# A spectral mixing layer times a gated GLU on one core: the first pair of GLU blocks by seven products, five pairs' first two products moved ahead, tokens 512-1023 by features, and one order table

## The chip, the core and the metric

The kernel runs on one core of one Trainium2 chip. The core has five engines with a queue each: TensorE (PE, matmuls, with its weight loads shown as PEld), VectorE (DVE), ScalarE (ACT), GpSimd (POOL) and SyncE (SP). SP and POOL issue nearly all DMA transfers. The metric is device time of one execution in microseconds (us); lower is better.

## What is computed

```
def _A_ref(x, ...):                       # x: 1 x 2048 x 512
    a = einsum("bsd,ed->bse", x, dft_hid_re)
    b = einsum("bsd,ed->bse", x, dft_hid_im)
    return einsum("ts,bse->bte", dft_seq_re, a) - einsum("ts,bse->bte", dft_seq_im, b)

def _B_ref(x, w_gate, w_up, w_down):      # F = 1792
    g = einsum("bsd,df->bsf", x, w_gate)
    u = einsum("bsd,df->bsf", x, w_up)
    return einsum("bsf,fd->bsd", sigmoid(g) * u, w_down)

xn = layernorm(x)
out = x + _A_ref(xn, ...) * silu(_B_ref(xn, w_gate, w_up, w_down))
```

All values are float32. The numbers S = 2048 tokens, D = 512 features, F = 1792 hidden columns.

## The kernel before, in words

**Precision.** Each matmul operand is split into a high part (ACT copies it to the matmul's reduced type, `split`, line 86) and a low part (DVE subtracts, line 87). A product is then three matmuls, high x high, high x low, low x high (`mm3`, lines 90 to 92), each 128 x 128 weights by up to 512 columns.

**Seven for eight.** A 2 x 2 block product is made of seven products of sums of blocks instead of eight of the blocks. The sums (lines 142 and 270) and the additions of results (`snap`, `plus`, `seed` in `block`) are work for DVE and ACT. A product number 1 to 7 names one of the seven, in the usual scheme: 1 and 2 use blocks as they are, 5, 6, 7, 3 and 4 use sums.

**The GLU.** F is cut into seven groups of 256 columns, g = 0 to 6, and the tokens into two halves, h = 0 and 1. A pair of a half and a group is a block of `BLOCKS`, fourteen with (0, 0). In `block` one product (`unit`) is 12 matmuls of 512 columns: two matrices (gate and up), two pieces of the contraction, three matmuls each. Banks of PSUM are named by matrix and chain: ga, ua, gb, ub, gc, uc, and two named pd. Behind a product stands one product of the earlier pair with w_down (`Seven.run`, six matmuls into pd); its result is copied by ACT and added in DRAM by a POOL transfer with accumulation (`gather`, lines 327 to 332, into g_part).

**The start.** The first pair, (0, 0), is not made by `block` but by `start` (line 520): eight products of the blocks themselves (`chunk`, line 541), with no sums of weights or x. Those on tokens 0-511 run in two halves of 256 columns. The tokens of the first half, 0-1023, are loaded in eight tiles of 128 (`fetch`), normalised (`norm_a` statistics, `norm_b`), transposed on PE (`turn`, line 231) and read out of PSUM three times (`keep_hi`, `keep_lo`, `keep_raw`). Filler matmuls on ones (`busy`) stand ahead of it. A string, `HEAD`, writes out the order of this part.

**The other tokens.** For tokens 1024-2047 x is not transposed. The host also passes x by features (x_t); the moments of the tokens go to DRAM (m_part), come back spread over all partitions, and DVE applies them (`turned_half`, line 217).

**Later stages.** After the fourteen pairs come the sequence DFT (`seq_units`), by seven products on two levels, and the hidden DFT with the gate (`hidden_units`).

**What sets the order.** Each queue runs in the order in which the program issues. Products are `units`; operands are loaded `LOAD_AHEAD` units ahead and split `SPLIT_AHEAD` ahead, or at places given by tables of offsets (S0, H0, S4, H4, LATE). Each page of SBUF has a home from a string, `HOMES`.

Of the kernel before, what the change touches and what calls it, by code (L numbers as in the profile page):

```python
# [15 lines left out]
P = 128  # L16
S, D, F = 2048, 512, 1792
NS = S // P
ND = D // P
# [7 lines left out]
BLOCKS = (*((0, g) for g in range(1, 7)), (1, 6), *((1, g) for g in range(6)))  # L27
# [3 lines left out]

HOMES = (
    "ab10cdiejfghZYXklmnoptqursvwxyzABCDEFGHIJKLMNOPQR1ST0XUVWoxmcftDwkplArsBnJzZISETYWHtRfmDylNAkvMQnBZE"
    "IzKLS0wWRCf1mXDyvckTnpZzESlRCJHtKm1MDQXNLcnBpYEZAzIKCyJ01QMLSpfXTBkzAEHtIlNJmMQvLpSRBDEkKIctNMfYLp0R"
    "BJ1DzAEXmcHMfCyYpLTlJ1AkQmXHC0SidTtMNAGFJDkzRfje0ESKTPOIdBcFVUQNyRxopknuqtlLIHfCB1AcFGvZQXjyRJnimkxz"
    "ICMYGD0ceuydJRviqZxmNCMBYt0GDRFdzJxcijqYMe0ntVURNdFDHfzuCcYqvI0MeyZDRfNJzBuCYIteGMiqjRDZdfFVvzYCHxIU"
    "etGnjRcdNz0FVYxMUyeBuCtncDNZdiHkFMfxJyqeBuvczDdHIMkJCeGqVYufvcNzZtxHiJk0enGqFfzDvtHmyiknqVfBOFPI0MtS"
    "DvEcHNYeTyKnagVZpfodOBuLlMqtmvJGAH10NxeXFnQZVzprwuBiKkGLJmvHjS0A1lDVZpxzwUkiGmJHvLAl1pxGiYzvHLUlGxSA"
    "YiHKvzlULRjxGtiYzvwbhASRNFLYisWwCbhAzYSDLscilFgbCOzAsLicFlfCgbodsiLwlFEobfiswFlAEowsfaFlTyAswaflLAyw"
    "slfSyAzsWwflyESYoszCwLWgflbEyiUdYFSTo0swzLvhgalfbWkUiEAyOSYDdCTcs0LzrhgkWiUDbYECdscL0kWUiEYrdfLCa0UW"  # L40
    "EDilrYAgyCa0EWkFliUAYDoygwE0sCkFfvilODYSyohwgs0ETfFiWvDOySkhwA0sCfTadiFYDvLUIPSyAbgwsCTfiMdqYFrnULQo"
    "cSPbOAewXgTCBfiuzvqdFZkVYInr0UJamLDoPOQybHKSslweCGTtXuiBEvq1pMAFdWjYgxVchLmyRNQHbs0rkKwlXCeEBvq1ZFAU"
    "SdMpPTmJLVgxaKkGf0QNszeCWtZ1dSOcIpnMPL"
)


@with_exitstack
def fnet_glu_kernel(ctx: ExitStack, tc: tile.TileContext, x, x_t, c_re, c_im, w_h, w_gu, w_down, out):
    nc = tc.nc
# [9 lines left out]
    def page(shape, dtype=F32R):  # L59
        return pages.tile([P, *shape], dtype, name="page", tag=next(homes))  # L60

    def bank(tag):
        return banks.tile([P, 512], F32, name=tag, bufs=2 if tag == "pd" else 1)

    ident = const.tile([P, P], F32, name="ident")
    make_identity(nc, ident)
# [6 lines left out]
    moments = const.tile([P, 2, 2, KH // 2], F32, name="moments")  # L73
# [4 lines left out]
    m_part = dram.tile([2, 2, P, KH // 2], F32, name="m_part")  # L78
# [103 lines left out]
    def norm_a(i):  # L182
        st = stats[:, i % 4, :]
        rs = stat.tile([P, 1], F32, name="rs")
        mv = moments[:, i % KH // 4, :, i % 4] if i >= KH else stat.tile([P, 2], F32, name="mv")
        nc.vector.bn_stats(st[:, :6], xs[i])
        nc.vector.bn_aggr(mv, st)
        mean, scale = mv[:, 0:1], mv[:, 1:2] if i >= KH else rs
        nc.gpsimd.tensor_tensor(scale, mv[:, 1:2], mhalf, op=ALU.pow)
        if i >= 4:  # L190
            nc.gpsimd.tensor_scalar(shifts[:, i - 4 : i - 3], mean, scale, -1.0, op0=ALU.mult, op1=ALU.mult)
        st_of[i] = mean, scale

    def second_norm(i):
        i_ = i - KH
        scale, bias = moments[:, i_ // 4, 1, i_ % 4 : i_ % 4 + 1], shifts[:, i - 4 : i - 3]
        nc.scalar.activation(xs[i], xs[i], AF.Identity, scale=scale, bias=bias)

    def norm_b(i):
        mean, scale = st_of.pop(i)  # L200
        if i >= 4:
            nc.scalar.activation(xs[i], xs[i], AF.Identity, scale=scale, bias=shifts[:, i - 4 : i - 3])
            return
        nc.vector.tensor_scalar(xs[i], xs[i], mean, scale, op0=ALU.subtract, op1=ALU.mult)

    def turned_half(n, b, at):

        both = Load(m_part[b].rearrange("m q o -> (m q o)").partition_broadcast(P).rearrange("p (m t) -> p m t", m=2), [2, SB])
        raw = [Load(x_t[(2 + b) * 2 + j], [2, SB]) for j in range(2)]

        def store():
            nc.gpsimd.dma_start(m_part[b].rearrange("m q o -> q m o"), moments[:, b])

        def step(j, m):
            v = xraw[1, j, b] = raw[j].load()
            by = both.load()[:, m, :].unsqueeze(1).to_broadcast([P, 2, SB])
            nc.vector.tensor_tensor(v, v, by, op=(SUB, ALU.mult)[m])

        after(n, store)
        sooner(at[0] - 2, both.load)  # L220
        for i in range(4):
            if i % 2 == 0:
                sooner(at[i] - 4, raw[i // 2].load)
            after(at[i], lambda i=i: step(*divmod(i, 2)))
# [3 lines left out]
    def turn(i):  # L228
        turned[i] = bank({2: "ga", 3: "ua"}.get(i, "pd")).rearrange("p (d s) -> p d s", d=ND)
# [62 lines left out]
    def w_operands(g):  # L292
# [19 lines left out]
        w["s"] = s1, s2, s3, s4  # L312
        return w
# [25 lines left out]
    HEAD = "C000 C001 C002 T2 S4 C010 H2 C011 T3 S5 H3 C012 R2 C100 C101 R3 N4 L2 L3 T4 u0 N5 H4 S6 R4 L4 C102 T5 S7 g00 R5 H5 C110 U0 N6 V0 L5 N7 T6 C111 d0 u1 C112 T7 H6 g01 p2 H7 L6 u2 L7 U1 h1 V1 m R7 R6 C200 x1 C201 C202 p3 C210 h2 X5 d1 g10 C211 u3 x2 d2 C212 d3 X6 g11"  # L339
    S0 = 8, 10, 8, 14  # L340
    H0 = 13, 11, 11, 12
    L4 = 9, 13, 15, 20
    S4 = 9, 7, 8, 12
    H4 = 8, 9, 11, 14
    X34 = 0, 0
    SEVEN_LAST = (1, 2, 6, 7, 4, 5, 3)
    waiting = []

    class Down:
# [22 lines left out]
        def spread(self, n, late):  # L372
            sooner(n + 4 * late - 4, self.wdl.load)
            for i, f in zip(LATE if late else (0, 2, 3, 5), (lambda: self.diffs(0), lambda: self.diffs(1), self.dif.get, self.raw.get)):
                after(n + i, f)

    class Seven:


        items, at = SEVEN, range(7)  # L380
# [18 lines left out]
        def spread(self, n, late):  # L399
# [3 lines left out]
            self.last = n == 7 * (len(BLOCKS) - 1)  # L403
            for i, v in zip(L4 if self.last else S0 if n < 0 else S4, self.sums):
                sooner(n + i, v.get)
            if not self.last:
                for i, v in zip(H0 if n < 0 else H4, (self.h[5], self.h[6], self.h[7], self.h[4])):
# [42 lines left out]
    def block(h, w, made, before, job, late, order=(1, 5, 2, 6, 7, 4, 3)):  # L450
# [3 lines left out]
        if not made:  # L454
            for i, v in zip((-2, -3, 0, 1), w["s"]):
# [25 lines left out]
        tail = {1: seed, 6: lambda: snap(2), 7: lambda: (snap(3), plus(3)), 3: lambda: plus(2)}  # L481
        CH = {1: "a", 5: "c", 2: "b", 6: "a", 7: "a", 4: "a", 3: "c"}

        def unit(k, d, parts=(0, 1)):
            first = k in (1, 5)
            for m in parts:
# [4 lines left out]
            if 1 not in parts:  # L491
                return
            if k in tail:
                tail[k]()
            if d:
                d[0].run(d[1])
# [7 lines left out]
        for i, k in enumerate(order):  # L504
            if i == 2:
                waiting.extend((before, d) for d in before.items)
            d = waiting.pop(0) if waiting and i in waiting[0][0].at else None
            add([xop[h, k], w[k]] + (d[0].needs(d[1]) if d else []), lambda *m, k=k, d=d: unit(k, d, m or (0, 1)))
        if order[1] == 2:
            job.product_two = lambda: times(1, "b")  # L510
        else:
            sooner(n + 3, lambda: times(1, "b"))
        sooner(n + 5, lambda: times(3))
        sooner(n + 7, lambda: times(2))
# [3 lines left out]
    following = []  # L518

    def start(h, g):  # L520

        loads = [Load(w_gu[g, k], [2, 4 * P]) for k in range(2)]
        down = Down(g)
        w, ps = {}, {}
        job = Seven(h, down, True)
        job.items = SEVEN_LAST
        job.spread(-7, False)

        def w_hi(f, j):
            k, o = QUAD[f, j]  # L530
            both = page([2, 4 * P])
            w[f, j] = both[:, 0], both[:, 1]
            nc.scalar.activation(both[:, 0], loads[k].load()[:, o, :], AF.Copy)

        def w_lo(f, j):
            k, o = QUAD[f, j]
# [698 lines left out]
```

## Time and profile before

| | |
|---|---|
| time, three runs (us) | 798.49, 799.17, 796.92; median 798.49 |
| span of the profiled execution (us) | 795.6 |
| PE clock granted | 1.00 throughout |
| HBM read, written (MB) | 104.86, 70.26 |
| POOL busy (us) | 121.9 (15%) |

The profile is of one execution. Its own whole time is not given beside it; the span runs from the first to the last instruction and is 2.9 us under the median. A busy share says how long an engine had work, not that the work was needed at once. Since PE stands at 99%, the rows to look at are PE's own pitch and, for the other engines, idle time in a stretch.

### The profile page before, as it was taken

How to read it: one execution, taken by the hardware profiler on the slowest of the kernel's cores; microseconds unless marked ns; L12 is line 12 of the kernel's file. 1: busy time of each engine (PE TensorE's matmuls, PEld its weight loads, DVE VectorE, ACT ScalarE, POOL GpSimd, SP SyncE). 2: the span in 40 equal slices, each digit the busy share in tenths (PEclk: the TensorE clock that was granted, in tenths of full speed). 3: DMA queues.
4: the chain of work that ended last, by engine and by line, in shares of the span. 5: the costliest groups of instructions: out<-in, count | busy, mean ns of one | idle time of the engine just before them, and what ended most of it. 6: DMA issues, size and time to landing. Idle time of an engine off the chain costs nothing.

```text
span 795.6 us, 10166 instructions
## 1 busy us (share of the span) xinstructions
PE 789.4 (99%) x3540; PEld 655.2 (82%) x3540; DVE 710.0 (89%) x925; ACT 543.6 (68%) x844; POOL 121.9 (15%) x173
## 2 busy tenths in 40 slices
PE   9999999999999999999999999999999999999997
PEld 8888888888888888888888888888888888888886
DVE  7899889899988988988988898899889899889987
ACT  5778888888877877978987747554544455449461
POOL 2003341111221312212110000101100000000102
PEclk9999999999999999999999999999999999999999
DMA  7058899887887899988998788829968684876836
GB/s 285 7 183 213 182 215 209 183 183 114 190 200 202 218 229 263 247 197 192 228 297 277 171 279 263 251 68 329 393 252 312 207 295 167 296 274 232 185 59 106
DMA packets 49571, 172.11 MB, mean 216 GB/s; under 512 B 5488, under 2 KB 5744, under 8 KB 49520
## 3 DMA queue, kind: packets, MB, share of 16 engines
q0 software_dynamic: 20128, 69.75, 41.7%
q1 hardware_dynamic: 29312, 101.66, 36.1%
q8 instruction: 27, 0.44, 0.2%
q14 instruction: 24, 0.20, 0.1%
q10 hardware_dynamic: 80, 0.07, 0.0%
HBM read 104.86 MB, written 70.26 MB: 220 GB/s over the span
## 4 chain that ended last, share of the span: by engine, by line
PE 99%; DVE 0%; ACT 0%; issue 0%
PE ga L91 6%; PE pd L91 6%; PE pd L92 6%; PE ga L92 6%; PE ga L90 6%; PE pd L90 6%; PE ua L92 6%; PE ua L91 6%; PE ua L90 6%; PE gb L92 4%; PE gb L91 4%; PE gb L90 4%; PE ub L92 4%; PE ub L91 4%; PE ub L90 4%; PE uc L92 4%
## 5 line engine op out<-in xcount | busy, mean ns | idle before, releaser
L87 DVE TENSOR_TENSOR page<-page 128x1024 fp32r<-128x1024 f32 (+2 forms) x408 | 370.8, 944 | 46.3 <-ACT page L86 44.9
L86 ACT ACTIVATE page<-page 128x1024 fp32r<-128x1024 f32 (+2 forms) x408 | 319.0, 834 | 130.4 <-DVE page L142 116.0
L142 DVE TENSOR_TENSOR page<-page 128x512 f32<-128x512 f32 (+2 forms) x280 | 223.9, 820 | 1.7
L327 ACT ACTIVATE page<-pd 128x512 f32<-128x512 f32 x140 | 81.9, 599 | 37.4 <-PE pd L92 31.8
L329 POOL DMA_DIRECT2D g_part<-page x76 | 65.7, 865 | 271.9 <-ACT page L327 244.7
L91 PE MATMUL ga<-page 128*128 128x512 f32 x200 | 77.9, 390 | 0.0
L91 PE MATMUL pd<-page 128*128 128x512 f32 x200 | 77.9, 390 | 0.0
L90 PE MATMUL ga<-page 128*128 128x512 f32 x200 | 77.9, 389 | 0.0
L92 PE MATMUL pd<-page 128*128 128x512 f32 x200 | 77.8, 389 | 0.0
L92 PE MATMUL ga<-page 128*128 128x512 f32 x200 | 77.8, 389 | 0.0
L90 PE MATMUL pd<-page 128*128 128x512 f32 x200 | 77.8, 389 | 0.0
L90 PE MATMUL ua<-page 128*128 128x512 f32 x196 | 76.3, 389 | 0.0
L91 PE MATMUL ua<-page 128*128 128x512 f32 x196 | 76.3, 389 | 0.0
L92 PE MATMUL ua<-page 128*128 128x512 f32 x196 | 76.2, 389 | 0.0
L90 PE MATMUL gb<-page 128*128 128x512 f32 (+1 forms) x140 | 53.7, 384 | 0.0
L92 PE MATMUL gb<-page 128*128 128x512 f32 (+1 forms) x140 | 53.6, 383 | 0.0
L91 PE MATMUL gb<-page 128*128 128x512 f32 (+1 forms) x140 | 53.6, 383 | 0.0
L91 PE MATMUL ub<-page 128*128 128x512 f32 x132 | 51.4, 389 | 0.0
L90 PE MATMUL ub<-page 128*128 128x512 f32 x132 | 51.4, 389 | 0.0
L92 PE MATMUL ub<-page 128*128 128x512 f32 x132 | 51.4, 389 | 0.0
L90 PE MATMUL gc<-page 128*128 128x512 f32 x124 | 48.2, 389 | 0.0
L91 PE MATMUL gc<-page 128*128 128x512 f32 x124 | 48.2, 389 | 0.0
(152 smaller groups left out, 1288.0 us busy)
## 6 DMA issues: line engine op xcount, KB each, us to landing
g_part<-page POOLq DMA_DIRECT2D x84, 512.0 KB, 6.3
page<-in_c_re_dram SPq DMA_DIRECT2D x49, 512.0 KB, 5.0
page<-in_c_im_dram SPq DMA_DIRECT2D x33, 512.0 KB, 5.6
page<-in_w_gu_dram SPq DMA_DIRECT2D x26, 512.0 KB, 5.5
f_part<-page POOLq DMA_DIRECT2D x16, 512.0 KB, 6.6
page<-f_part SPq DMA_DIRECT2D x16, 512.0 KB, 4.7
page<-i_part SPq DMA_DIRECT2D x14, 512.0 KB, 4.5
page<-in_w_down_dram SPq DMA_DIRECT2D x13, 512.0 KB, 4.9
```

The costliest lines, as they stand in the source:

```text
L86: nc.scalar.activation(hi, src, AF.Copy)
L87: nc.vector.tensor_tensor(lo, src, hi.bitcast(F32), op=SUB)
L90: nc.tensor.matmul(ps, ws[0], ms[0], start=first, stop=False, skip_group_check=go_on)
L91: nc.tensor.matmul(ps, ws[0], ms[1], start=False, stop=False, skip_group_check=go_on)
L92: nc.tensor.matmul(ps, ws[1], ms[0], start=False, stop=last, skip_group_check=go_on)
L142: (engine or nc.vector).tensor_tensor(dst, a, b, op=op)
L327: nc.scalar.activation(pg[:, o, :], po, AF.Copy, scale=float(sign))
L329: nc.gpsimd.dma_start(g_part[i], pg, accum_op=ADD)
```

## The change

It has five parts.

1. The pair (0, 0) becomes an ordinary block of `BLOCKS`, made by seven products. `start` and its `chunk` over eight products go.
2. For the first `AHEAD` = 5 pairs, products 1 and 2 are made ahead of all others, by a new class `Ahead`. They need only tokens 0-511. For pairs 0 and 1 they run in halves of 256 columns, as the tiles arrive. The result of product 1 is kept in SBUF (`keep`; for pair 0 in its bank) and put back into bank ga and ua by ACT after product 5 (`again`). These five pairs then have five units each (`SHORT`).
3. The products with w_down of the first pairs are put off: `COUNTS` says how many follow each unit, none at first, then one and two in turn.
4. Tokens 512-1023 are taken from x by features, as those of the second half were (`Turned`). Their moments go through m_part too; their token order within the block changes as in the other blocks, on the host (`columns`).
5. The kernel records every instruction (`Recorder`, `Ref`) and issues them in the order of one table of numbers (`ORDER`, `emit`). `HOMES` is new as well. All instructions of the changed kernel therefore have one line, that of `emit` (L326).

```diff
-BLOCKS = (*((0, g) for g in range(1, 7)), (1, 6), *((1, g) for g in range(6)))
+BLOCKS = (*((0, g) for g in range(7)), (1, 6), *((1, g) for g in range(6)))
+AHEAD = 5
...
+0 15-16 72 5 20 3 31 1 6 4 19 7 9 21 8 11 29 13 10 22 12 14 74 23 32 73 24 26 33 25 36 27 30 108 28 35 176
...
+def emit(program, order):
...
+    for part in order.split():
+        first, _, last = part.partition("-")
+        for f, a, k in program[int(first) : int(last or first) + 1]:
+            f(*map(found, a), **{n: found(v) for n, v in k.items()})
...
+        def step(self, j, m):
+            h, b = divmod(self.q, 2)
+            v = xraw[h, j, b] = self.raw[j].load()
+            by = self.both.at[:, m, :].unsqueeze(1).to_broadcast([P, 2, SB])
+            nc.vector.tensor_tensor(v, v, by, op=(SUB, ALU.mult)[m])
...
+    SHORT = 5, 6, 7, 3, 4
+    COUNTS = "00000 00012 12121 21212 21212 1111111 1111111"
...
+        def again():
+            for m, c in enumerate("gu"):
+                if kept.g == 0:
+                    ps[c + "a"] = kept.ps[1][m]
+                else:
+                    ps[c + "a"] = bank(c + "a")
+                    nc.scalar.activation(ps[c + "a"], kept.first[:, m, :], AF.Copy)
...
+    class Ahead:
...
+        BANK = "a", "c", "b", "c", "pd"
...
+        def chunk(self, k, n, q):
+            at = (slice(0, 2 * P), slice(2 * P, SB), slice(0, SB))[q]
...
+            for m in range(2):
+                for kt in range(2):
+                    o = (2 * m + kt) * P
+                    nc.tensor.matmul(
+                        self.ps[k][m][:, at],
+                        self.w[k].at[u][:, o : o + P],
+                        xop[0, k].at[v][:, kt, at],
...
+        def keep(self, q):
...
+            for m in range(2):
+                to = self.first[:, m, at] if self.g else self.ps[2][m][:, at]
+                nc.scalar.activation(to, self.ps[1][m][:, at], AF.Copy)
...
-            d = waiting.pop(0) if waiting and i in waiting[0][0].at else None
+            d = [waiting.pop(0) for _ in range(min(len(waiting), counts[n + i] if n + i < len(counts) else 1))]
...
-    def start(h, g):
...
+        emit(program, ORDER)
```

Where it moves instructions, three places. PE first, from the filler matmuls on (ones) over the transposes of the first two token tiles (ident) to the first useful products. Before:

```order
L569 MATMUL gc<-ones 128x512 x10
L231 MATMUL pd<-ident,page 128x128 x4
L569 MATMUL gc<-ones 128x256 x2
L231 MATMUL pd<-ident,page 128x128 x4
L569 MATMUL gc<-ones 128x256 x4
L550 MATMUL gb<-page 128x256 x2
L550 MATMUL ub<-page 128x256 x2
```

The same place after the change, from the last of the ten wide fillers on:

```order
L326 MATMUL ub<-ones 128x512 x3
L326 MATMUL pd<-ident,page 128x128 x4
L326 MATMUL gb<-ones 128x256
L326 MATMUL pd<-ident,page 128x128 x4
L326 MATMUL ua<-page 128x256 x2
L326 MATMUL ub<-ones 128x256
L326 MATMUL gb<-ones 128x256 x2
L326 MATMUL ub<-ones 128x256
L326 MATMUL ua<-page 128x256 x2
L326 MATMUL ga<-page 128x256 x6
L326 MATMUL ub<-ones 128x256
L326 MATMUL gc<-page 128x256 x2
```

One narrow filler now stands ahead of the first useful product instead of six; the others stand between useful ones.

ACT, from the start of the program to the reads of the third and fourth token tile (pd to page are reads of a transposed tile, page to page splits of weights). Before:

```order
L72 ACT_TABLE_LOAD
L72 ACTIVATE warm<-mhalf 128x1
L533 ACTIVATE page<-page 128x512
L250 ACTIVATE page<-pd 128x2x128 x4
L533 ACTIVATE page<-page 128x512 x3
L242 ACTIVATE page<-pd 128x2x128 x4
L250 ACTIVATE page<-ga 128x2x128 x2
L250 ACTIVATE page<-ua 128x2x128 x2
```

After:

```order
L326 ACT_TABLE_LOAD
L326 ACTIVATE page<-page 128x512 x2
L326 ACTIVATE page<-pd 128x2x128 x5
L326 ACTIVATE page<-page 128x512
L326 ACTIVATE page<-pd 128x2x128
L326 ACTIVATE page<-page 128x512
L326 ACTIVATE gb<-ga 128x256
L326 ACTIVATE ub<-ua 128x256
L326 ACTIVATE page<-pd 128x2x128 x2
L326 ACT_TABLE_LOAD
L326 ACTIVATE warm<-mhalf 128x1
L326 ACTIVATE page<-pd 128x2x128 x6
```

The load for the sigmoid, which stood first, is now a second load behind the reads of the first two tiles; copies that seed bank gb and ub stand ahead of it.

DVE, at the place where tokens 512-1023 become operands. Before, it takes their low parts out of PSUM, tile by tile (pd):

```order
L256 TENSOR_TENSOR page<-pd,page 128x2x128 x2
L87 TENSOR_TENSOR page<-page 128x512
L256 TENSOR_TENSOR page<-pd,page 128x2x128 x2
L87 TENSOR_TENSOR page<-page 128x512
L479 TENSOR_TENSOR page<-page,ub 128x512
L270 TENSOR_TENSOR page<-page 128x1024
```

After, it applies the moments to the pages loaded by features (here with the tiles' numbers: 392 holds the moments, 295 and 312 the two halves of x) and goes on to sums of x:

```order
L326 TENSOR_TENSOR page_312<-page_312,page_392 128x1024
L326 TENSOR_TENSOR page_295<-page_295,page_392 128x1024
L326 TENSOR_TENSOR page_312<-page_312,page_392 128x1024
L326 TENSOR_TENSOR page_295<-page_295,page_392 128x1024
L326 TENSOR_TENSOR page_483<-page_312,page_181 128x1024
```

Eight reads in pieces of 2 x 128 columns became four operations of 1024, behind a wait for m_part's way through DRAM; over the whole program DVE has 5 operations of 1024 columns and 11 of 512 more, and 8 of 2 x 128 fewer.

More of the change, by code (lines that the diff above doesn't have):

```diff
@@ L312, in w_operands @@
         w["s"] = s1, s2, s3, s4
+        w["loads"] = loads
         return w
@@ new lines, in fnet_glu_kernel @@
+    job = last = None
+    ahead = []
+    for h, g in BLOCKS:
+        made = g == last
+        if not made:
+            w, wd, last = w_operands(g), Down(g), g
+        new = Seven(h, wd, made)
+        kept = None
+        if len(ahead) < AHEAD:
+            kept = Ahead(g, w, new.s)
+            ahead.append(kept)
+        order = STEADY if not kept else SHORT if g < AHEAD - 1 else (5, 6, 7, 4, 3)
+        job = block(h, w, made, job, new, (h, g) != BLOCKS[-1], order, kept)
+    for i, f in zip(X0, (lambda: x_sum(0, 3), lambda: x_sum(0, 4), xop[0, 7].get, xop[0, 3].get, xop[0, 4].get)):
+        sooner(i, f)
```

651 lines of the change are left out of this document (434 added, 217 removed).

## Prediction

> **What bounds the kernel now.** I read the page's busy shares and chain first, then the PE waits, then the PE timeline of the opening and of the end, and last the windows, for the engine that stands second.
>
> ```profile
> span 795.6 us, 10166 instructions
> PE 789.4 (99%) x3540; PEld 655.2 (82%) x3540; DVE 710.0 (89%) x925; ACT 543.6 (68%) x844; POOL 121.9 (15%) x173
> PE 99%; DVE 0%; ACT 0%; issue 0%
> PE gc L569 <- DVE ones L68: 1.4, 1, 1.4
> ```
>
> PE is busy for 99% of the span, the chain of work is PE alone, and its only named wait is the first 1.4 us. So time goes where matmuls go, as long as nothing new makes PE wait. The rows of the PE timeline (start, length, instruction) give the pitches and the few waits that are there.
>
> ```profile
> 6.58 0.78 PE L569 MATMUL gc<-ones 128*128 128x256 f32 x2
> 7.16 0.69 PE L231 MATMUL pd<-ident,page 128*128 128x128 f32 x4
> 7.60 0.72 PE L569 MATMUL gc<-ones 128*128 128x256 f32 x4
> 8.32 0.50 PE L550 MATMUL gb<-page 128*128 128x256 f32 x2
> 8.66 0.39 PE L550 MATMUL ub<-page 128*128 128x256 f32 x2
> 9.11 0.50 PE L550 MATMUL gb<-page 128*128 128x256 f32 x2
> ...
> 17.57 0.60 PE L231 MATMUL pd<-ident,page 128*128 128x128 f32 x4
> 17.92 0.48 PE L550 MATMUL gb<-page 128*128 128x256 f32 x2
> 18.24 0.40 PE L550 MATMUL ub<-page 128*128 128x256 f32 x2
> 18.48 0.40 PE L550 MATMUL gb<-page 128*128 128x256 f32 x2
> ...
> 20.35 0.40 PE L90 MATMUL ga<-page 128*128 128x512 f32 x1
> ...
> 50.66 0.49 PE L91 MATMUL pd<-page 128*128 128x512 f32 x1
> 50.98 0.40 PE L92 MATMUL pd<-page 128*128 128x512 f32 x1
> ```
>
> ```profile
> 778.85 0.39 PE L92 MATMUL ub<-page 128*128 128x512 f32 x1
> ...
> 785.20 0.28 PE L90 MATMUL gb<-page 128*128 128x256 f32 x1
> ...
> 790.69 0.28 PE L92 MATMUL gb<-page 128*128 128x256 f32 x1
> ```
>
> - A 512-wide matmul: 28 begin between 778.85 and 785.20, so 0.2268 us each. A 256-wide pair takes 0.24 (18.24 to 18.48), so 0.12 each.
> - Four transposes: from 17.57 the second pair behind them begins at 18.24; less one pair that is 0.43.
> - Waits of PE now: from 8.32 to 20.35 are 40 pairs (9.6) and four groups of transposes (1.72), together 11.3 of 12.0 us: 0.7 of waits, two of them visible (9.11 instead of 8.90) and one more of 0.1 at 50.66. Over everything from 8.32 to the last matmul at 790.69, 3372 x 0.2268 + 120 x 0.12 + 6 x 0.43 leaves the same 0.8.
>
> The windows show who stands second (columns: window, its length, busy time of PE, PEld, DVE, ACT, POOL with counts, clock, DMA share, GB/s).
>
> ```profile
> 0.00:20.00 20.00, 18.47 (x118) 16.71 (x119) 14.44 (x36) 11.86 (x31) 5.68 (x18) 1.00 0.79 284
> 20.00:40.00 20.00, 20.00 (x104) 16.99 (x103) 17.72 (x31) 15.16 (x30) 1.14 (x4) 1.00 0.02 7
> 40.00:60.00 20.00, 20.00 (x89) 16.32 (x88) 19.15 (x29) 14.83 (x27) 1.84 (x3) 1.00 0.54 184
> 60.00:80.00 20.00, 20.00 (x90) 16.55 (x89) 19.42 (x34) 17.37 (x31) 7.71 (x11) 1.00 0.88 213
> 80.00:100.00 20.00, 20.00 (x90) 16.55 (x89) 17.36 (x31) 16.74 (x29) 5.86 (x8) 1.00 0.88 184
> ```
>
> DVE is idle for 5.6, 2.3, 0.9, 0.6 and 2.6 us: 11.9 us in the first 100, of which 3.0 lie before its first data.
>
> ```profile
> 3.45 0.69 DVE L186 BATCH_NORM_STATS2 stats<-page 128x6 f32<-128x512 f32 x1 [2.06 <-DMA page<-in_x_dram]
> 110.03 0.69 DVE L142 TENSOR_TENSOR page<-page 128x512 f32<-128x512 f32 x1
> 110.64 0.69 DVE L479 TENSOR_TENSOR page<-page 128x512 f32<-128x512 f32 x1
> 782.41 2.35 DVE L87 TENSOR_TENSOR page<-page 128x1024 fp32r<-128x1024 f32 x2
> ```
>
> DVE operations follow each other at 0.60 us (512 wide) and 1.13 (1024 wide, 2.35 less 1.22 of the last).
>
> **What goes from PE.** Seven products of 12 matmuls stand where eight stood: 12 x 0.2268 = 2.7 us. Tokens 512-1023 are no longer transposed: four groups at 0.43 = 1.7 us. Counted in the two orders that is 3540 matmuls to 3512, and the 120 of 256 columns stay 120. Together **4.4 us**. The end of the program, from the last pieces of the output on, stands in PE's queue as before: nothing there.
>
> **What comes back, the fillers.** Before, all six 256-wide filler matmuls ran ahead of the first useful one (6.58, 7.60), where PE waited anyway. Now five of the six stand behind it: 5 x 0.12 = **0.6 us**, if PE has work there; nothing, if they fill waits of the next paragraph, so I count them once. The start itself I leave at 8.3: it hangs on the second transpose and one read by ACT, as before. ACT now splits a second weight block ahead of them, inside the time in which it would wait for that transpose.
>
> **What comes back, the opening.** Here ACT is the short engine.
>
> ```profile
> 6.25 0.63 ACT L533 ACTIVATE page<-page 128x512 fp32r<-128x512 f32 x1 [4.03 <-DMA page<-in_w_gu_dram]
> 7.88 0.66 ACT L250 ACTIVATE page<-pd 128x256 fp32r<-128x256 f32 x2 [0.26 <-PE pd L231]
> 9.70 1.41 DVE L256 TENSOR_TENSOR page<-pd,page 128x256 fp32r<-128x256 f32 x4
> 10.40 1.15 ACT L533 ACTIVATE page<-page 128x512 fp32r<-128x512 f32 x2 [1.35 <-DMA page<-in_w_gu_dram]
> 493.64 1.28 ACT L947 ACT_TABLE_LOAD   x1
> 495.05 2.22 ACT L86 ACTIVATE page<-page 128x1024 fp32r<-128x1024 f32 x2
> ```
>
> A read of a transposed tile takes 0.33, a weight split 0.63, and where ACT and DVE read one bank they take turns (0.35 each). I lay ACT's queue end to end from 7.9. The copy that seeds product 2 of the first pair follows six reads and two splits and ends at 11.0; PE, with 16 useful matmuls and five fillers since 8.3 (21 x 0.12), is there at 10.8: a wait of 0.3 with the signal. Then ACT loads a table in mid-stream; the second load of before shows its price, 493.64 to 495.05 = 1.4 us with the small activation behind it. The tiles of tokens 256-511 are read behind it at 14.7, PE wants them at 14.2: 0.5. The copy of pair 1's first product ends at 15.9, PE is there at 15.4: 0.5. With a few restarts of 0.1 that is 1.5 us of waits against 0.7 now: **0.8 us** back.
>
> On that table load the Trainium skill ("ScalarE: Activation LUTs", What ACT_TABLE_LOAD costs) says about 1.28 us and then a drain of about 1.38, so 2.66 for a switch of sets. The trace agrees with the 1.28 and shows no drain: the next wide activation begins 1.41 after the load. By the page the third wait would be 1.4 us longer, and the sum the same amount less good; I go by the row.
>
> **What must be covered: DVE.** By the order, DVE gets 5 more operations of 1024 columns (x by features: subtract and multiply), 11 more of 512 (weight sums and splits of the first pair) and 8 fewer of 256: 5 x 1.13 + 11 x 0.60 - 8 x 0.34 = 9.5 us, nearly all in the first 100 us, where 11.9 - 3.0 = 8.9 were idle after the first data. So the cover is the whole idle time of DVE. I added DVE's queue up to each operand that PE waits for. After 98.7 us of products PE needs an operand that stands 103.9 us deep in DVE's queue, 103.3 of it behind 3.45. PE is there at 8.3 + 98.7 + 1.5 = 108.5, so DVE has 105.05 us: 1.75 to spare, and the turns with ACT in the opening take 1.6 of it. The same margin, 0.1 to 0.5 us, stands at some twenty places between 24 and 108 us. For before the same sum has 42.7 us of queue for the matmul at 50.66, plus 7.9 idle by the windows (none between 40 and 50): 50.6, and that row shows PE waiting 0.1. The sum can be trusted to some tenths.
>
> So each further wait of DVE there is a wait of PE, though not added up: the longest lateness counts. Who can be late are transfers.
>
> ```profile
> g_part<-page POOLq DMA_DIRECT2D x3, 512.0 KB, 6.0
> DMA to landing us min/median/max: 2.0/3.7/7.2
> ```
>
> The first row is the issues from 60 to 70 us, median to landing; the second is all four transfers of m_part. Between the first gather and the ACT instruction that waits for its page stand 22 matmuls, 5.0 us: about 1 us late by the 6.0. The moments of tokens 512-1023 leave POOL at about 20.7 by the same laying out; store and load at the median end at 20.7 + 3.7 + 3.7 = 28, wanted by DVE at 29.3; a load of 7.2 would be 2.3 late. Of all this I take **0.4 us**, between nothing and 3: most landings are covered by ACT's lead. The three added loads (two of x_t, one of m_part) and POOL's store stand in the DMA's empty time (0.02 from 20 to 40).
>
> **Sum.** -4.4 + 0.6 + 0.8 + 0.4 = -2.6 on a span of 795.6. The median of the runs is 2.9 above the span, which stays. 798.5 - 2.6 = **795.9 us**, 0.33% less.
>
> **Rivals.**
> - *Little is given back.* The fillers lie in the waits, the loads that are no longer held back land sooner, DVE is never late: -4.4 + 0.3 = 794.4. For it: x and weights are issued in one row from 0.7 on. Against it: ACT's queue is long whatever the loads do. Chance 0.20.
> - *DVE's cover breaks.* A moments transfer 2.3 late, or gathers 1.5 to 3 late, stop DVE inside its full stretch: -3.0 + 2.5 = 798.0. For it: margins of tenths over 80 us. Against it: with 0.88 of the DMA taken from 60 to 100, nearly all the idle time ahead of DVE's largest group is put down to ACT (row below), none to a transfer. Chance 0.19.
> - *The table load holds ACT longer* where it stands in the opening, by as much again as the load itself (1.28): 795.9 + 1.3 = 797.2. Against it the row at 495.05. Chance 0.04. The Trainium skill's drain is this case.
> - *The gathers choke: slower.* The deferred last products run 23 in 15 units of the third to fifth pair (15 x 2.72 + 23 x 1.36 = 72 us), 3.1 us apart, where before had one per 4.1. The last but one gather of a pair and the first of the next write the same part of g_part, and POOL, in order, waits for the earlier to land: two gathers on, 6.2 us. With a landing over 6.2 it waits; at the 8.2 of the row below it is 2 us at each of four joints. If pages and pd banks are held that long, PE stops 8 us less the cover of 1: 795.9 + 7 = 803. It decides from a landing of some 7 us on. For it: 8.2 has been seen. Against it: with 8.2 PE did not wait. Chance 0.09.
>
> ```profile
> L87 DVE TENSOR_TENSOR page<-page 128x1024 fp32r<-128x1024 f32 (+2 forms) x408 | 370.8, 944 | 46.3 <-ACT page L86 44.9
> ...
> g_part<-page POOLq DMA_DIRECT2D x2, 512.0 KB, 8.2
> ```
>
> (The second row is the issues from 100 to 110 us.)
>
> That the change does not do what it says I exclude: the matmuls are counted in the order.
>
> **How the numbers follow.** Forecast 0.48, 795.0 to 796.8. With 0.20 at 794.4, 0.23 at 797 to 798.6 and 0.09 at 803, a range from 793.8 to 798.6 leaves out the last and little more. Faster by over 0.3% (about what a measurement of this kernel can tell from none) means under 796.1: all of 794.4 and two thirds of the forecast, 0.52. Slower by over 0.3% is 0.09; the rest, 0.39, is within.
>
> **What would show it.** PE has 3512 matmuls and, behind 8.3, under 2 us of idle, all before 25 us; DVE is 97% busy from 20 to 108 and the PE waits name DVE there with tenths. The first useful matmul stands at 8.3. If PE's waits name DVE with more than 2 us in all, the cover was the error; if idle POOL time shows g_part in long pieces and PE waits for pd, the gathers; if the opening's waits on ACT are over 2, the table load or the loads' crowding. If the last matmul begins before 787 I gave back too much.

## The result and the profile after: 2.7% slower

| | before | changed |
|---|---|---|
| median (us) | 797.88, 4 runs | 818.22, 4 runs (817.83 to 821.73) |
| ratio to before | | 1.0267, interval 1.0245 to 1.029 |
| span of the profiled execution (us) | 795.6 | 816.3 |
| first useful matmul, begin of the last (us) | 8.32, 790.69 | 8.28, 788.91 |

The forecast was 795.9 us, and the range ended at 798.6. The page of the changed kernel answers to the rows of before (span, share of the engines, chain of work):

```profile
span 816.3 us, 10116 instructions
PE 786.3 (96%) x3512; PEld 650.7 (80%) x3512; DVE 716.3 (88%) x933; ACT 543.0 (67%) x851; POOL 126.4 (15%) x174
PE 90%; DVE 3%; DMA 2%; ACT 1%; POOL 1%; issue 1%; POOLq 0%; SPq 0%; DVEq 0%; ACTq 0%
```

PE has 3.1 us less busy time and ends earlier, as forecast, yet its share of the span falls from 99% to 96%. So PE's queue did not get longer: the span did, behind it. The windows of the end (window, length, busy time of PE, PEld, DVE, ACT, POOL with counts, clock, DMA share, GB/s) show the changed kernel's last 76 us:

```profile
740.00:760.00 20.00, 20.00 (x90) 16.58 (x89) 19.19 (x19) 9.47 (x11) 0.00 (x0) 1.00 0.07 27
760.00:780.00 20.00, 20.00 (x89) 16.55 (x89) 15.99 (x17) 11.55 (x14) 0.00 (x0) 1.00 0.00 1
780.00:800.00 20.00, 9.18 (x52) 7.89 (x50) 8.52 (x14) 0.00 (x0) 7.92 (x8) 0.78 0.36 67
800.00:816.00 16.00, 0.00 (x0) 0.00 (x0) 0.00 (x0) 0.00 (x0) 1.26 (x2) 0.50 0.99 179
```

For 40 us the DMA engines stand nearly still, and POOL does nothing. Then the DMA is 0.99 busy for 16 us in which no engine computes. The granted clock of 0.78 and 0.50 stands only where PE has nothing left to do; up to 789 us, where PE starts its last matmul, it is 1.00. What moves so late, POOL's timeline says (start, length, instruction, idle time ahead and what ended it). The kernel before:

```profile
737.61 1.24 POOL L1056 DMA_DIRECT2D out_dram<-page  x1 [19.19 <-DVE page L1047]
744.13 1.21 POOL L1056 DMA_DIRECT2D out_dram<-page  x1 [5.28 <-DVE page L1055]
...
782.79 1.20 POOL L1056 DMA_DIRECT2D out_dram<-page  x1 [3.38 <-DVE page L1055]
786.39 0.90 POOL L1050 DMA_DIRECT2D out_dram<-page  x1 [2.40 <-DVE page L1049]
787.80 0.87 POOL L1050 DMA_DIRECT2D out_dram<-page  x1 [0.51 <-DVE page L1096]
```

The changed kernel:

```profile
715.48 0.56 POOL L326 DMA_DIRECT2D f_part<-page  x1 [11.22 <-ACT page L326]
792.08 9.18 POOL L326 DMA_DIRECT2D out_dram<-page  x8 [76.04 <-DVE page L326]
```

Before, the eight stores that add a block to `out` left one by one from 737.6 on. Now all eight stand in one row from 792.1 on: POOL waited 76 us for the first. Its queue in the changed kernel, with the pages' numbers, shows why:

```
168 DMA f_part<-page_6430 128x1024
169 DMA out<-page_6851 128x512      (second half of the last but one block)
170 DMA out<-page_6629 128x2x512    (before: the first store of all)
171 DMA out<-page_6572 128x2x512
172 DMA out<-page_6823 128x2x512
173 DMA out<-page_6544 128x2x512
174 DMA out<-page_6745 128x2x512
175 DMA out<-page_6917 128x2x512
176 DMA out<-page_6851 128x512      (first half of the last but one block)
```

Row 169 waits for page 6851. Of the six whole blocks behind it the first is done at about 737 us, and five are done 8 us or more before 6851; they wait. The input of row 169 is itself late, as DVE's timeline of the changed kernel shows:

```profile
789.22 0.42 DVE L326 TENSOR_TENSOR page<-page,gb 128x256 f32<-128x256 f32 x1 [3.75 <-PE gb L326]
789.55 1.02 DVE L326 TENSOR_TENSOR page<-page 128x256 f32<-128x256 f32 x2
790.49 0.68 DVE L326 TENSOR_TENSOR page<-page,ub 128x512 f32<-128x512 f32 x1
791.09 1.62 DVE L326 TENSOR_TENSOR page<-page 128x512 f32<-128x512 f32 x3
792.63 0.68 DVE L326 TENSOR_TENSOR page<-page,pd 128x512 f32<-128x512 f32 x1
```

Before, the multiplications of this block stood at 785.39 and 786.72. Now the one that row 169 needs is the first of the three at 791.09, behind a row that waits 3.75 us for PE's very last bank; and a multiplication out of a pd bank, whose last matmuls start at 750.77 by PE's timeline, comes last of all. In the order table these entries (nine of them: 5315, 5349, 5388, 5424, 5557, 5588, 5619 and 5622 for POOL, 5423 for DVE) stand at its end. None is waited for by anything but a store or the end of the program.

### The profile page after: what moved, and what is told of

The parts are those of the page before. It is cut to its first block, busy times and chain, and to the rows that moved or that the text cites. A ratio compares the mean times of both kernels' runs of the same rounds, so it can differ in the third digit from the quotient of the medians.

```text
span 816.3 us, 10116 instructions
## 1 busy us (share of the span) xinstructions
PE 786.3 (96%) x3512; PEld 650.7 (80%) x3512; DVE 716.3 (88%) x933; ACT 543.0 (67%) x851; POOL 126.4 (15%) x174
## 4 chain that ended last, share of the span: by engine, by line
PE 90%; DVE 3%; DMA 2%; ACT 1%; POOL 1%; issue 1%; POOLq 0%; SPq 0%; DVEq 0%; ACTq 0%
PE ga L326 16%; PE pd L326 16%; PE ua L326 16%; PE gb L326 11%; PE gc L326 11%; PE ub L326 11%; PE uc L326 11%; DVE page L326 3%; DMA g_part<-page 1%; POOL out_dram L326 1%; ACT page L326 1%; DMA page<-in_w_gu_dram 1%; DVE stats L326 0%; POOL moments L326 0%; ACT L326 0%
## 5 line engine op out<-in xcount | busy, mean ns | idle before, releaser
L326 DVE TENSOR_TENSOR page<-page 128x512 fp32r<-128x512 f32 (+5 forms) x756 | 628.0, 889 | 56.0 <-ACT page L326 47.5
L326 ACT ACTIVATE page<-page 128x512 fp32r<-128x512 f32 (+3 forms) x452 | 350.3, 823 | 130.5 <-DVE page L326 109.2
L326 PE MATMUL pd<-page 128*128 128x512 f32 x624 | 158.9, 390 | 0.1
L326 PE MATMUL ga<-page 128*128 128x512 f32 (+1 forms) x606 | 156.7, 387 | 0.2 <-ACT page L326 0.2
L326 PE MATMUL ua<-page 128*128 128x512 f32 (+1 forms) x594 | 154.0, 387 | 0.9 <-ACT page L326 0.9
L326 PEld LDWEIGHTS pd<-page 128*128 128x128 f32 x624 | 116.9, 188 | 25.5 <-ACT page L326 1.3
L326 PEld LDWEIGHTS ga<-page 128*128 128x128 f32 x606 | 113.2, 188 | 23.6 <-ACT page L326 0.4
L326 PEld LDWEIGHTS ua<-page 128*128 128x128 f32 x594 | 110.9, 188 | 24.1 <-ACT page L326 1.2
L326 POOL DMA_DIRECT2D g_part<-page x84 | 70.5, 862 | 317.1 <-ACT page L326 293.8
L326 ACT ACTIVATE page<-pd 128x512 f32<-128x512 f32 (+2 forms) x161 | 89.6, 577 | 36.0 <-PE pd L326 30.9
L326 PE MATMUL gc<-page 128*128 128x512 f32 (+1 forms) x420 | 110.8, 384 | 0.1
L326 PE MATMUL uc<-page 128*128 128x512 f32 (+1 forms) x420 | 110.4, 383 | 0.0
L326 PE MATMUL gb<-page 128*128 128x512 f32 (+1 forms) x420 | 109.6, 381 | 0.2 <-ACT gb L326 0.2
L326 PE MATMUL ub<-page 128*128 128x512 f32 (+1 forms) x396 | 105.9, 386 | 0.0
L326 PEld LDWEIGHTS gc<-page 128*128 128x128 f32 x420 | 78.0, 188 | 16.1 <-ACT page L326 0.6
L326 PEld LDWEIGHTS uc<-page 128*128 128x128 f32 x420 | 77.9, 188 | 15.6 <-DVE page L326 0.2
L326 PEld LDWEIGHTS gb<-page 128*128 128x128 f32 x420 | 76.9, 188 | 15.8 <-ACT gb L326 0.8
L326 PEld LDWEIGHTS ub<-page 128*128 128x128 f32 x396 | 73.8, 188 | 15.0
L326 ACT ACTIVATE page<-ga 128x512 f32<-128x512 f32 x51 | 30.5, 597 | 12.2 <-PE ga L326 11.5
L326 POOL DMA_DIRECT2D f_part<-page x16 | 8.9, 558 | 176.8 <-DVE page L326 152.1
L326 ACT ACTIVATE page<-gb 128x512 f32<-128x512 f32 x32 | 19.1, 596 | 24.1 <-PE gb L326 23.2
L326 ACT ACTIVATE page<-ua 128x512 f32<-128x512 f32 x36 | 21.5, 598 | 9.3 <-PE ua L326 9.1
```

Source lines behind the costliest of these rows:

```text
L326: f(*map(found, a), **{n: found(v) for n, v in k.items()})
```

## Experiments

In all of them the time from the begin of PE's last matmul to the end of the span is called the tail: 795.6 - 790.7 = 4.9 us before, 816.3 - 788.9 = 27.4 after. PE's own length is taken from the first useful matmul to the begin of the last: 780.62 us in the changed kernel, and 780.57 to 780.64 in three of the four versions that differ from it only at the end, so one execution shows a change of some 0.2 us. The one line of all instructions is L316 or L317 in the versions of the changed kernel, since the table's text is some lines shorter there.

### All late entries back in place

The entries of the order table for the last blocks go back to where their inputs are ready; all else stays. Two of the eight stores, a multiplication and the end of the table:

```diff
-... 5332 5314 5321 5352 ...
+... 5332 5314 5315 5321 5352 ...
-... 5422 5425 5421 5433 ...
+... 5422 5425 5421 5423-5424 5433 ...
-... 5653-5665 5636 5618 5650 5621 5651 5622 5666 5423 5315 5667-5668 5637 5388 5652 5588 5349 5424 5557 5619
+... 5653-5668
```

> The changed kernel, with the entries of its order table for the last output blocks put back to where their inputs are ready: the eight stores into out by POOL, the last multiplications by DVE behind their matmuls, the three stores by SP. Nothing else is moved. Theory A (the whole loss is the tail: PE ends earlier than before, and POOL's queue holds seven finished output blocks behind one store that waits for the last DVE work): the last matmul still begins at about 788.9 and the tail behind it becomes that of the kernel before, 795.6 - 790.7 = 4.9 us, so a span of 793.8 and a time 22.5 us under the changed kernel's, about 795.7, a ratio of 0.997 to the kernel before. Rival B (accumulating stores have become slower by themselves, 13.0 us to landing against 6.1, through the places of pages or the fills of out with x): the span stays over 805. Rival C (what the DVE queue lost in the tail is as large as what the stores lost): this run can't tell it from A, the next two can.

Measured: 795.43 us against 797.86 for the kernel before on the same chip (12 and 17 runs), a ratio of 0.9975, interval 0.9963 to 0.9987. The page's span, and the first and last of POOL's eight stores:

```profile
span 793.9 us, 10122 instructions
...
736.95 1.23 POOL L316 DMA_DIRECT2D out_dram<-page  x1 [20.69 <-DVE page L316]
...
786.10 0.86 POOL L316 DMA_DIRECT2D out_dram<-page  x1 [0.56 <-DVE page L316]
```

The last matmul begins at 789.1, the tail is 4.8 us. Span and tail come within 0.1 us of theory A, and rival B is out: with the places of the pages unchanged, the 512 KB stores land 6.2 us (median) behind their issue, as before (6.1), not 13.0. One detail of the expectation was wrong: the held store keeps back five finished blocks, not seven, for the sixth and the other half block come late from DVE. This version is faster than the kernel before, by 0.25%.

### One of the two alone

Either only DVE's entries go back (5423, 5618, 5621, 5635, 5636, 5650, 5651), or only POOL's eight stores, each behind its DVE instruction as the table has that.

```diff
 DVE alone:
-... 5650 5621 5651 5622 5666 5423 5315 ...
+... 5622 5666 5315 ...
 POOL alone:
-... 5665 5636 5618 5650 5621 5651 5622 5666 5423 5315 5667-5668 5637 5388 5652 5588 5349 5424 5557 5619
+... 5665 5636 5618-5619 5650 5621-5622 5651 5666 5423-5424 5667-5668 5637 5652
```

> The changed kernel with only the DVE entries of the tail put back behind their matmuls; the eight POOL stores stay in one row at the end, the first still waiting for the second half of the last but one block. Theory A: the first store starts when that half is multiplied, about 784.8 instead of 792.1, and the row of eight then takes as long as it did, 24.2 us, so the span is about 809. Rival C (DVE's late work is the loss): 794 to 796.

> The changed kernel with only the eight POOL stores put where their inputs are ready; DVE keeps its late order, so five stores of 512 KB leave early and three (256, 256 and 512 KB) leave behind 790.5, 791.8 and 793.3. Theory A with a price by volume (4.0 MB in the 24.2 us behind 792.1, so 6 us for each MB): 1.0 MB by POOL and 0.45 by SP and ACT behind 792, about 9 us, a span of 800 to 802. Rival C: 812 or more. If the price is the landing of the last store alone (13.0): 806.

Measured: spans of 813.0 and 803.6, ratios to before of 1.0188 (1.016 to 1.0216) and 1.0088 (1.0065 to 1.0111). In the first, POOL's row begins at 788.03 and takes 25.0 us to the end; here PE's last matmul begins 2.3 us later than in the changed kernel. Of these, 1.1 are there at the first useful matmul (9.34), because the first weights landed late (below), and 1.3 are lost in the opening behind it, where the granted clock was 0.57 from 9 to 13 us (columns as in the windows above; the version with all in place has 1.00 there):

```profile
9.00:13.00 4.00, 3.66 (x18) 3.66 (x19) 3.65 (x10) 2.93 (x9) 1.10 (x2) 0.57 1.05 416
```

In the second, the last three stores:

```profile
791.22 0.91 POOL L317 DMA_DIRECT2D out_dram<-page  x1 [7.79 <-DVE page L317]
792.42 0.86 POOL L317 DMA_DIRECT2D out_dram<-page  x1 [0.29 <-DVE page L317]
794.27 1.20 POOL L317 DMA_DIRECT2D out_dram<-page  x1 [0.99 <-DVE page L317]
```

Against each run's last matmul the tails are 21.8 and 14.3 us, with 27.4 for both faults and 4.8 for none. So of 22.6 us the row of stores makes 13.1 and DVE's late work 9.5, taken off in that order (17.0 and 5.6 in the other). Rival C falls as these two runs put it (DVE's work as the whole loss): neither is the whole. Both guesses of the size were too low, by 4 and by 2 us. Of the 4, 2.3 are PE's lateness, 0.9 a release of the first store that I had put too early (788.0 less 2.3 is 785.7, not 784.8), and 0.8 a longer row (25.0 us, not 24.2). The other execution of that version has a span of 809.6, 0.6 over the guess.

### The same fault put into the kernel before

In the kernel before, four of the eight stores are held until the second half of the last but one block is stored. The first three stay, since later pages use the places of theirs.

```diff
-nc.gpsimd.dma_start(to, r, accum_op=ADD)
+held.append(lambda: nc.gpsimd.dma_start(to, r, accum_op=ADD))
+if (pair, k) in [(0, 2), (0, 7), (0, 3)]:
+    held.pop()()
...
+if halves and d:
+    for f in (held[-1], *held[:-1]):
+        f()
```

> The kernel before, with four of its eight POOL stores into out held back in the queue: the fourth to sixth block and the first half of the last but one leave behind the second half of the last but one, at about 787.8. Nothing is moved on PE, DVE and ACT. Theory A, by volume: 2.0 MB by POOL and 0.45 by SP and ACT behind 787.8 at 6 us for each MB are 14.7 us, so the span goes from 795.6 to about 802.5, 0.9% slower than before. Rival D (stores that stand in a row at the end are hidden, and the loss has its cause elsewhere): 795 to 796.5.

Measured: a span of 806.4 us and a median time of 808.3, ratio 1.0125 (1.0107 to 1.0144); the tail is 15.4 us instead of 4.9. The fault alone makes the kernel before 1.3% slower, so rival D is out. The price was too low again (802.5 expected). With the other runs it can be corrected. From the first store of the last row to the end: 24.2 us for 3.67 MB by POOL in the changed kernel, 18.3 for 2.10 MB here (788.10 to 806.4), 12.4 for 1.05 MB with the stores in place (791.22 to 803.6). From the first to the last of these that is an estimated 4.5 us for each MB on top of 7.7, where I had 6 us for each MB and nothing on top. The row in between lies 1.2 us over that line, so it is good to about a microsecond.

### Held stores that write instead of add

The changed kernel as it is, but the eight stores write their block (the addition of x is left out).

```diff
-nc.gpsimd.dma_start(to, r, accum_op=ADD)
+nc.gpsimd.dma_start(to, r)
```

> The changed kernel as it is, its eight POOL stores in one row at the end, but each writes its block into out instead of adding it (the addition of x is left out). Theory R1 (the adding sets the 204 GB/s of the row, since loads by SP moved 390): the row of 24.2 us shrinks to 13 to 16, a span of 805 to 808. Rival R2 (the stores' number, their rows of 2 KB or POOL's issuing set the rate): 815 to 817.

Measured: a span of 806.9, ratio 1.0143 (1.0123 to 1.0163); R1's forecast holds. Packets and MB of POOL's queue, and issues to landing, in the DMA view of the end, changed kernel first, then this one:

```profile
q0 software_dynamic: 1920, 3.67, 64.3%
...
out_dram<-page POOLq DMA_DIRECT2D x6, 512.0 KB, 13.0
```

```profile
793.09 5.36 POOL L317 DMA_DIRECT2D out_dram<-page  x8 [76.03 <-DVE page L317]
...
q0 software_dynamic: 1024, 3.67, 28.0%
...
out_dram<-page POOLq DMA_DIRECT2D x6, 512.0 KB, 6.4
```

The row takes 793.1 to 806.9, 13.8 us instead of 24.2, and moves 377 to 437 GB/s in its second half where adding moves 191 to 214. So 10.4 us of the 24.2 go with the adding. That the adding itself sets the rate is not shown: the plain stores also went in fewer packets (1024 for the same 3.67 MB, against 1920), and no run separates the two. Of rival R2, the number of stores and POOL's issuing are out; the size of the pieces is not. The Trainium skill ("DMA: Bandwidth & Descriptors", Anatomy of one DMA — SWDGE (gpsimd) path) gives about 2 us and the bytes at 436 GB/s for a transfer; by that the row, taken as one transfer, is an estimated 10.4 us. The plain row comes near that rate in its second half, the adding one goes at half of it.

### More work for DVE, early and late

The version with all in place; two subtractions of 1024 columns at 42 us, or four of 512 at 227 us, are done twice.

```diff
-... 347 ... 366 ...
+... 347 347 ... 366 366 ...
```

> The kernel of e1 (all stores in place), with two of DVE's subtractions of 1024 columns at about 42 us done twice: 2 x 1.13 = 2.3 us more on DVE, no other work. Theory D (the idle time of DVE up to 108 us is used up, and DVE is what PE waits for at 109, 117 and 125 us): nearly all of it comes out on PE, whose waits between the first wide matmul and 136 us go from 1.3 us to 2.8 to 3.6; the last matmul begins 1.5 to 2.3 later than in e1, taken from the first useful one. Rival G (those waits hang on transfers and on ACT, and DVE still has a lead of its own): waits of 1.3 to 1.8.

> The kernel of e1, with four of DVE's subtractions of 512 columns at about 227 us done twice: 4 x 0.60 = 2.4 us more on DVE, as in the run before, but where DVE idles for 4.5 us in a stretch of 20. All theories: nothing on PE, the last matmul within 0.2 of e1's, taken from the first useful one. If PE is later by 1 us or more here too, DVE's idle time is no cover and theory D falls.

Measured early: 798.28 us, ratio 1.0007 (0.9997 to 1.0016), against 0.9975 without. PE's first two new waits:

```profile
44.74 1.42 PE L316 MATMUL ga<-page 128*128 128x512 f32 x5 [0.57 <-DVE page L316]
...
49.47 1.65 PE L316 MATMUL gc<-page 128*128 128x512 f32 x6 [0.57 <-DVE page L316]
```

The last matmul begins 3.1 us later behind the first useful one. 2.2 of it stands between 44 and 53 us, in waits that name DVE: nearly the whole 2.3 us came out on PE at once. Another 0.7 stands at 126.5 and is not DVE's: PE waits there for ACT, which had been idle for a gather (a transfer into g_part):

```profile
124.92 1.06 ACT L316 ACTIVATE page<-page 128x1024 fp32r<-128x1024 f32 x1 [1.21 <-DMA g_part<-page]
```

The waits up to 136 us went from 1.3 to 4.2, above what theory D expected, and rival G is out: DVE has no time left at 44 us. The old waits at 109, 118 and 134 us did not grow (0.29, 0.15 and 0.12, 0.29, as without). So theory D was wrong that PE waits for DVE there; the next run shows what it waits for. Measured late (one execution): 0.7 us, mostly one wait of 0.6 for DVE at 243.6, where nothing was expected. DVE's idle time there ended with waits for ACT, so not all of it was free.

### Two gathers less

The version with all in place without two of the transfers into g_part (entries 917 and 926).

> The kernel of e1 without two transfers with accumulation into g_part at 106 and 112 us (their part of the w_down product is left out). Theory G1 (the wait of 0.41 before the matmul at 124.8 comes from the landing of the gather issued at 111.9, 9.7 us, through the page that ACT writes next, as the chain of the trace has it): this wait falls under 0.1, the others stay, and PE ends 0.3 to 0.4 earlier. Rival D1 (ACT waits there for DVE, as the row of ACT's own idle time says): 0.35 to 0.45 as before.

Measured (one execution): PE's wait stays, 0.33 us where it was 0.39 by the starts of the matmuls. It stands inside a row of twelve matmuls into pd, ahead of the seventh. ACT and that seventh matmul with all in place:

```profile
121.68 1.06 ACT L316 ACTIVATE page<-page 128x1024 fp32r<-128x1024 f32 x1 [0.44 <-DVE page L316]
122.65 0.57 ACT L316 ACTIVATE page<-pd 128x512 f32<-128x512 f32 x1
123.28 1.65 PE L316 MATMUL pd<-page 128*128 128x512 f32 x6
```

Without the two gathers:

```profile
120.68 1.05 ACT L316 ACTIVATE page<-page 128x1024 fp32r<-128x1024 f32 x1
122.10 0.60 ACT L316 ACTIVATE page<-pd 128x512 f32<-128x512 f32 x1 [0.37 <-PE pd L316]
122.75 1.66 PE L316 MATMUL pd<-page 128*128 128x512 f32 x6
```

Neither theory holds. The gather did hold ACT (0.44 idle, gone without it), though the row names DVE, but it made only 0.06 of PE's wait. PE waits for ACT's read of a pd bank, which ends at 123.22 and 122.70, and goes on 0.05 behind it. The twelve matmuls are two products with w_down in a row, and there are two pd banks: the seventh needs the bank that PE finished three matmuls (0.68 us) earlier, and ACT's read of it takes 0.6 and starts only when PE has finished it. That is a round trip between PE and ACT; only what ACT is late beyond it is the gather's.

### The opening: fillers and the table load

Three versions of the one with all in place (the first two with one execution each): without the five fillers behind the first useful matmul (entries 18 and 53 to 56), with the sigmoid's table first (entry 2 ahead of entry 35), and both.

> The kernel of e1 without the five fillers of 256 columns that stand behind the first useful matmul. In e1 the first wide matmul begins 14.43 us behind the first useful one: 96 narrow matmuls 11.5, five fillers 0.6, transposes 0.9, waits 1.45. Theory F0 (ACT's queue sets the opening, the fillers lie in its shadow, so they should not have been charged besides the waits): still 14.3 to 14.45, the waits grow by 0.6. Theory F1 (the prediction's: 0.6 us of PE work on the path): 13.8 to 13.9.

> The kernel of e1 with the small sigmoid activation as ACT's first entry, so that its table is loaded at 0.7 us, before any data is there, as in the kernel before, and no second load stands in the opening. Theory T (the load, 1.4 us with its activation, delays the reads of the tiles of tokens 256-511, and causes the two waits of 0.3 at 14.5 and 15.7): they go, and the first wide matmul begins 13.8 to 13.9 behind the first useful one instead of 14.43. Rival (those waits hang on the transposes or on DVE): 14.4. If the wait were to move on behind the reads: 14.1.

> The kernel of e1 with the sigmoid's table first and without the five fillers. F0 and T together: 13.8 to 13.9 from the first useful to the first wide matmul, last matmul 780.0 behind the first useful one, a time 0.6 us under e1's, a ratio of 0.9968 to the kernel before. F1 and T: 13.2 and 0.996. Neither T nor F1: as e1, 0.9975.

From the first useful to the first 512-wide matmul: 14.43 us, 14.32 without fillers, 13.99 with the table first, 13.73 with both. F0 holds: taking 0.6 us of fillers away gains 0.1, the waits take the rest. T holds for 0.4 of 0.6; the two waits at 14.5 and 15.7 are gone, a new one of 0.2 appears at 10.4. ACT with all in place, where the load stands in mid-stream:

```profile
11.76 0.66 ACT L316 ACTIVATE page<-pd 128x256 f32<-128x256 f32 x2
12.44 1.28 ACT L316 ACT_TABLE_LOAD   x1
13.73 0.20 ACT L316 ACTIVATE warm<-mhalf 128x1 f32<-128x1 f32 x1
13.84 1.74 ACT L316 ACTIVATE page<-pd 128x256 fp32r<-128x256 f32 x6
```

From the load to the next read are 1.40 us, as priced. The drain of 1.38 that the Trainium skill ("ScalarE: Activation LUTs", What ACT_TABLE_LOAD costs) adds does not appear: the last read ends at 12.42, the small activation starts 1.29 behind the load's start.

At the end little is left of it. The last matmul begins 780.58 us behind the first useful one with all in place, 781.25 without fillers, 780.39 with the table first, 780.24 with both; what PE gained early it waits for later. In the run without fillers that is 1.0 us at 123.5, at the same round trip as above, with ACT held by a gather ahead of it:

```profile
121.87 1.06 ACT L316 ACTIVATE page<-page 128x1024 fp32r<-128x1024 f32 x1 [1.19 <-DMA g_part<-page]
```

The version with both has a ratio of 0.9973 (0.9964 to 0.9982), not to be told from 0.9975.

## Why the prediction was wrong, step by step

**The step that failed** is the sentence "The end of the program, from the last pieces of the output on, stands in PE's queue as before: nothing there." Its first half is true, and the conclusion does not follow. I had compared the end on PE alone. On POOL and DVE the order of the last blocks was another, and it stood in the order of the changed kernel for anyone to read. The cost is 22.6 us of tail, shown by taking the cause out (4.8 us of tail left), by halves, and by putting it into the kernel before. "That the change does not do what it says I exclude" was argued from the same count of matmuls.

The rival that ended slower was another one, choking gathers at 803 us, and it did not happen at that size: POOL waited 13.1 us in all for earlier transfers into g_part, but no wait of PE on the list names a gather, and what a gather cost PE through ACT is under 0.1 us in the changed kernel and at most 0.8 in any version.

With the tail in place, the rest of the sum can be judged: 795.43 against 797.86 is -2.4 us by the times, 793.9 against 795.6 is -1.7 by the two profiled spans, where -2.6 was forecast. That 795.43 comes so near to the forecast of 795.9 is in part luck: PE gave back 0.9 us more than was priced, and the "2.9 above the span, which stays" did not stay; the two errors nearly cancel. Time less span is 1.7 to 1.9 in 38 executions of the changed order, and 1.7 to 3.0 in 47 of the kernel before (median 1.9). The steps below go by the profile of the changed kernel. Its PE timeline at the two ends of the opening and at three waits:

```profile
8.28 0.50 PE L326 MATMUL ua<-page 128*128 128x256 f32 x2 [0.91 <-ACT page L326]
...
22.70 1.09 PE L326 MATMUL gb<-page 128*128 128x512 f32 x4
...
106.48 2.50 PE L326 MATMUL pd<-page 128*128 128x512 f32 x9
108.82 1.53 PE L326 MATMUL gc<-page 128*128 128x512 f32 x6
...
121.37 3.24 PE L326 MATMUL pd<-page 128*128 128x512 f32 x12
124.44 1.52 PE L326 MATMUL ga<-page 128*128 128x512 f32 x6
...
131.24 2.50 PE L326 MATMUL pd<-page 128*128 128x512 f32 x9
133.58 1.53 PE L326 MATMUL ga<-page 128*128 128x512 f32 x6
```

Nine matmuls from 106.48 on end their pitch at 108.52 (9 x 0.2268), and the next begins at 108.82: a wait of 0.30 inside the row. The waits of this kind are too short for the list of waits to name most of them. ACT's reads of pd at three of the places, and PE's seventh matmul of the row of twelve, show who makes them:

```profile
107.36 0.60 ACT L326 ACTIVATE page<-pd 128x512 f32<-128x512 f32 x1 [0.72 <-PE pd L326]
116.51 0.58 ACT L326 ACTIVATE gb<-pd 128x512 f32<-128x512 f32 x1 [0.22 <-PE pd L326]
122.30 0.60 ACT L326 ACTIVATE page<-pd 128x512 f32<-128x512 f32 x1
122.95 1.66 PE L326 MATMUL pd<-page 128*128 128x512 f32 x6
```

- *PE's work, -4.4:* 3512 matmuls, as counted. From the first useful to the last matmul the distance fell from 782.37 to 780.63, -1.7; so 2.7 us came back on PE, where 1.8 were priced. (The kernel before with held stores, which has the same matmuls, needs 783.07, with one wait of 0.4 at 519 us; by that one it would be 2.0.)
- *Fillers +0.6 and opening +0.8:* together 1.35 measured (14.42 us less 96 x 0.12 and 0.86 of transposes are 2.04, fillers in, against 0.7). The sum was right, the parts weren't: the fillers cost 0.1, and the waits without them are 1.9.
- *Start at 8.3:* 8.28. But it hangs on something else now. With two weight splits ahead of the reads, the first useful matmul begins 1.75 us behind ACT's first split (6.53 here), and that split waits for the first weights. Over the runs of the changed order it began at 8.04 to 9.34.
- *DVE cover, +0.4:* the wait was the wrong one, and its size too. That DVE's time is used up was right: 87.05 of the 88 us from 20 to 108. But PE has no wait over 0.1 us from 24 to 107, so nothing made DVE late enough for PE to wait. What came instead is 1.2 us from 107 to 134 (0.30, 0.27, 0.35, 0.30 by the rows), four waits for ACT to read a pd bank: PE goes on at 108.01, 117.14, 122.95 and 132.77, and ACT's reads end at 107.96, 117.09, 122.89 and 132.72. Three stand where two products with w_down follow each other directly, which came with the put-off products (part 3 of the change; the kernel before has no such row); the other (117.14) is a bank gb that ACT fills from pd. The prediction has no term for this. The three at 108, 117 and 133 come out alike, to 0.02, in the changed kernel and in all its versions. The one at 123 has the same floor and grows by what a gather holds ACT: to 1.0 with more work for DVE ahead and without fillers, and a little with both changes of the opening (0.5).
- *What would show it:* under 2 us of idle behind 8.3 failed (2.8), "all before 25" too, "97% busy" held (99%), and the waits name ACT, not DVE.

## What to carry to other kernels

Where a change moves instructions by a table, compare the end of every queue, stores first: an instruction that nothing waits for costs nothing until the end, and there it costs all at once. A finished store behind an unfinished one on the same in-order queue is a late store; ask of the last instructions of each engine when their inputs are ready, and whether they are issued then. An idle DMA in the last stretch of a kernel that has output left is the sign to look for in the profile. And where products are moved together, count the banks: one that is needed again three matmuls later (0.68 us here) is not yet read out by an engine that takes 0.6 and starts behind the last matmul.

## What was not expected of the hardware

A row of stores that add in DRAM moved about 204 GB/s with the DMA engines 0.99 busy, the same row without adding 377 to 437 in its second half, in about half as many packets; what of this is the adding and what the packets is open. 2.3 us more work on DVE, where it was busy nearly all the time, delayed PE by 2.2 at once; 2.4 us in a stretch with 4.5 us of idle time still by 0.7.
